# Taps of a depthwise convolution as products on ScalarE and accumulating DMAs, in a kernel of back-to-back matmuls

## The chip, the cores and the metric

The kernel runs on one core of one Trainium2 chip. Five engines of the core matter here, each with its own in-order queue of instructions: TensorE (PE, matmuls, with its weight loads listed as PEld), VectorE (DVE), ScalarE (ACT), GpSimd (POOL) and SyncE (SP, which here only issues DMAs). DMAs can be issued from SP's, ScalarE's and GpSimd's queues; they run on 16 DMA engines that all queues share.

The metric is the device time of one execution in microseconds. The kernel before takes 2484.3 us in the median of 9 runs (2483.25 to 2486.72).

## The reference

Two stages follow each other. `x` is 8 x 4096 x 192, float32; there are 8 heads of 24 channels and 7 taps.

```python
w = softmax(weight, axis=-1)                  # 8 heads x 7 taps
x_pad = concatenate([zeros(B, 6, D), x], 1)   # causal padding of 6 rows
attn[b, s, c] = sum_k w[head(c), k] * x_pad[b, s + k, c]

x2 = attn.reshape(32768, 192)
h = x2 @ w_in                                 # 192 x 2048
g = h * (1 / (1 + exp(-h)))                   # SiLU
out = g @ w_out                               # 2048 x 192
```

The first stage is a small sum of seven shifted and scaled copies of `x` along the sequence. The second is a pair of matrix products over 32768 tokens, and holds nearly all the arithmetic.

## The kernel before, in words

**Blocks and chunks.** The tokens are cut into 32 blocks (`NB`) of 1024. Within a block, the two halves of 512 tokens lie side by side on the partitions: partitions 0 to 63 hold 64 channels of the first half, partitions 64 to 127 the same channels of the second half. The 192 channels are three chunks (`k` = 0, 1, 2) of 64. So a chunk of a block is one tile of 128 partitions x 512 float32, 2 KB a partition.

**From x to the input of the matmuls.** Five steps make the operands of a block:

- `load` (line 123): 12 DMAs on SP bring `x` into the tile `nat`, with tokens on partitions.
- `turn_in` (tokens `i.k` of the plan, line 303): a 32 x 32 block transpose on VectorE, chunk by chunk, from `nat` into `xt`. After the third one, SP issues a small DMA `xt<-xt` that gives the second half its six rows of padding (line 309); GpSimd copies the first half's padding from `tail` (line 300).
- `conv` (tokens `v.ki`: chunk k, tap i; lines 315 to 327): the taps. Tap 0 writes `xt` times the tap's weight into `nat`, whose contents have been transposed already; taps 1 to 6 multiply the shifted `xt` and add to `nat`. All 21 of a block are on VectorE.
- `spread` (line 335): four DMAs a chunk on SP copy each half of `nat` to both halves of the partitions of `dup`, 128 KB each.
- `win` (tokens `w.0` to `w.3`, line 353): four differences of parts of `dup` on VectorE, into `win`.

**The two products.** The kernel saves multiplications with a scheme of the Strassen-Winograd kind over two halves of the tokens, two halves of the hidden columns and two chunks of the channels; the third chunk is multiplied plainly. In the up phase of a block (`product`, line 409), for each of eight column groups m, 11 products go into three PSUM banks. The plan calls them P1 to P7 and E11 to E22, with `P5.0` meaning product P5 of group 0. P1, P6, P7, P4 and E21 add up in one bank, which is read after P1 (`s1`), after P6 (`s2`) and after P7 (`s3`); these copies (`sums_h`, line 424) go to tiles `u`. `C11`, `C12`, `C22` (line 433, VectorE) add a copy and a bank into `g`; `g..` tokens apply SiLU in place (line 430, ScalarE); `C21` is a SiLU straight from the bank (line 428, ScalarE). In the down phase (`down`, line 464), `g` and differences of `g` (`t.ji`, line 450, VectorE) are multiplied by `w_out`. `merge` (tokens M, y, z and c, lines 547 and 550) puts the five result banks together, on ScalarE and VectorE, in `cmb`; `turn_out` (`o.i`, line 559) transposes on VectorE, and four stores a chunk (line 566) follow.

**What sets the order.** The order is written out by hand in `PLAN`: 88 slots separated by `|`, 44 for the up phase and 44 for the down phase, each with two matmuls of TensorE and the work of other engines beside them. `pin` keeps these instructions in the program's order on their engine; the framework adds the waits that data and buffers call for, and places the DMAs and GpSimd's instructions, which are not pinned. Tokens i, v and w in the plan of block b work for block b + 1. A leading minus means the block before. `nat`, `xt`, `dup` and `win` have one buffer each, so `spread` waits until the up phase has read the old `dup`, and `load` for block b + 2 waits until `spread` has read `nat`.

**The first block.** Block 0 is different. Its weights are still being converted from float64 bit patterns by `rounded` on VectorE (line 109), its up phase is plain (`up_plain`, line 373) and its down phase too (`down_plain`, line 503, followed by three copies into `cmb` on ScalarE, line 516). The tokens i, v and w of block 0's plan, which prepare block 1, come in the program after the last call of `rounded` and, those of the second half, within `down_plain`.

Of the kernel before, what the change touches and what calls it, by code (L numbers as in the profile page):

```python
# [9 lines left out]
F32 = mybir.dt.float32  # L10
I32 = mybir.dt.int32
AF = mybir.ActivationFunctionType
ALU = mybir.AluOpType
# [4 lines left out]
def kernel(  # L18
# [24 lines left out]
    nc = tc.nc  # L43
# [6 lines left out]
    P = 128  # L50
    R = 64
    NK = D // R
    grp = D // H
    pad = K - 1
    TB = 512
# [12 lines left out]
    xpool = ctx.enter_context(tc.tile_pool(name="xp", bufs=1))  # L68
# [9 lines left out]

    PLAN = (
        "P1.0 P1.1 -z7.0 -M3.0 | P1.2 P5.0 s1.1 -M4.0 | P5.1 E22.0 s1.0 -M5.0 s1.2 | "  # L80
        "E22.1 P6.1 -M6.0 | P6.0 P1.3 s2.1 | P6.2 P5.2 -o.0 s1.3 s2.0 | P5.3 P7.1 s2.2 | "
        "P7.0 E22.2 -o.1 s3.1 | P7.2 P6.3 i.0 s3.0 C22.1 | E22.3 E21.1 s3.2 s2.3 | "
        "P4.0 P4.1 g22.1 C22.0 | E12.1 P7.3 C22.2 g22.0 | E21.0 E12.0 i.1 C21.1 s3.3 i.2 | "
        "E21.2 E12.2 C21.0 C22.3 | P3.1 P3.0 g22.2 | P4.2 P4.3 g22.3 C12.0 | "
        "E12.3 P2.0 C12.1 g12.0 | P2.1 E11.0 v.00 C21.2 v.01 g12.1 | E11.1 E21.3 C11.0 | "
        "P1.4 P1.5 v.02 C21.3 | P1.6 P3.2 g11.0 C11.1 s1.4 | P3.3 P5.4 C12.2 s1.5 | "
        "P6.4 E22.4 s1.6 C12.3 g11.1 | P5.5 P6.5 s2.4 g12.2 | E22.5 P1.7 v.03 g12.3 s2.5 | "
        "P7.4 P2.2 s1.7 v.04 | P6.6 E11.2 s3.4 v.05 | P2.3 P7.5 C22.4 | "
        "P4.4 P6.7 s2.6 s3.5 C11.2 | E11.3 E12.4 g22.4 s2.7 g11.2 | P7.6 E21.5 C22.5 | "
        "E21.4 P7.7 C11.3 s3.6 | P3.5 P4.5 v.06 g22.5 s3.7 t.00 | E21.6 P3.4 C21.4 | "  # L90
        "E12.5 P4.7 C21.5 t.01 | P4.6 P2.4 g11.3 C12.4 | P5.7 E11.4 C21.6 C12.5 | "
        "E22.7 E21.7 g12.4 C11.4 g12.5 | P2.5 P5.6 C22.7 C21.7 | E11.5 E22.6 t.03 g11.4 | "
        "E12.7 P2.6 g22.7 C22.6 | P3.7 E11.6 C11.5 g22.6 | P2.7 E12.6 v.10 g11.5 C11.6 | "
        "E11.7 P3.6 C12.7 g11.6 | C11.7 g12.7 | C12.6 g11.7 v.11 | g12.6 t.02 | . | v.12 | "
        "v.13 v.14 | v.15 | v.16 | v.20 | t.10 | t.11 | . | t.13 | v.21 | v.22 | v.23 | "
        "t.12 | v.24 | v.25 | v.26 | t.20 | t.21 | . | t.23 | t.22 | t.30 | . | t.31 | w.0 | "
        "w.1 | w.2 | w.3 | t.33 | t.32 | . | . | . | cE.0 | o.2 | y1.0 | z1.0 z6.0 | "
        "z4.0 M2.0 | M1.0 | z5.0"
    )

    def pin(ins):
        return tc.keep_in_program_order(ins)
# [8 lines left out]
    vec = Pinned(nc.vector)  # L111
# [6 lines left out]
    def load(b):  # L118
# [12 lines left out]
        out=wexp.rearrange("p h k -> p (h k)"),  # L131
        in_=weight.rearrange("(o h) k -> o (h k)", o=1).to_broadcast([P, H * K]),
# [5 lines left out]
    for k in range(NK):  # L138
        nc.gpsimd.dma_start(
            out=xts[0][R:P, k, 0:pad], in_=x0[:, k, :], allow_slow_non_contiguous=True  # L140
# [116 lines left out]
    for e in range(2):  # L257
        half = hot[R * e : R * e + R]
        for sign, base in ((1, 0), (-1, grp - 1)):
            nc.gpsimd.affine_select(  # L260
                out=half,
                in_=half,
# [50 lines left out]

    def conv(b, k, i):

        src = xts[b][:, k, i : i + TB]
        dst = nats[b][:, k, :, :].rearrange("p k c -> p (k c)")
        tap = taps[:, k, i : i + 1]
        if i == 0:
            pin(nc.vector.tensor_scalar(dst, src, scalar1=tap, scalar2=None, op0=ALU.mult))  # L320
        else:
            pin(
                nc.vector.scalar_tensor_tensor(  # L323
                    out=dst, in0=src, scalar=tap, in1=dst, op0=ALU.mult, op1=ALU.add
                )
            )

    def spread(b, k):
# [86 lines left out]
    def g_of(b, m, a, n):  # L415
        return g_tile(b, m // 2, a)[:, n, m % 2, :]

    def sums_h(b, name, m):


        if name[0] == "s":
            u = us[b, m, name[1]] = upool.tile([P, TB], F32, tag="u", name="u")
            copy = nc.vector.tensor_copy if name == "s2" else nc.scalar.copy
            pin(copy(u, bk[b, m, "1"]))  # L424
            return
        g = g_of(b, m, int(name[1]) - 1, int(name[2]) - 1)
        if name == "C21":
            pin(nc.scalar.activation(g, bk[b, m, "1"], AF.Silu))  # L428
        elif name[0] == "g":
            pin(nc.scalar.activation(g, g, AF.Silu))  # L430
        else:
            i, bn = {"C11": ("1", "b"), "C22": ("3", "d"), "C12": ("2", "d")}[name]
            pin(nc.vector.tensor_tensor(g, us.pop((b, m, i)), bk[b, m, bn], op=ALU.add))  # L433
# [140 lines left out]
    def step(b, token):  # L574

        if token[0] == "-":
            b, token = b - 1, token[1:]
        name, arg = token.split(".") if "." in token else ("", "")
        if b < 0 or b >= NB or not name or (b, token) in did:
            return  # L580
        did.add((b, token))
        digits = [int(c) for c in arg]
        if name[0] in "PE":
            product(b, digits[0], name)
        elif name[0] in "sCg":
            if b:
                sums_h(b, name, digits[0])
        elif name == "t":
            sum_g(b, *digits)
        elif name[0] in "Mzyc":  # L590
            merge(b, name)
        elif name == "o":
            turn_out(b, *digits)
        elif b + 1 < NB:
            {"i": turn_in, "v": conv, "w": win}[name](b + 1, *digits)
            if name == "v" and digits[1] == K - 1 and (b, "down") in did:
                spread(b + 1, digits[0])
                if digits[0] == NK - 1 and b + 2 < NB:
                    load(b + 2)
# [13 lines left out]
    for k in range(NK):  # L613
        turn_in(0, k)
        for i in range(K):
            conv(0, k, i)
        spread(0, k)
        if k == 0:
            round_in(0)
            load_in(2, nc.gpsimd)  # L620
# [69 lines left out]
```

## Time and profile before

| | |
|---|---|
| median of 9 runs | 2484.3 us (2483.25 to 2486.72) |
| the profiled execution | 2483.94 us, of which the span of the profile is 2482.2 us |
| granted TensorE clock, mean | 0.998 |
| TensorE busy | 2444.1 us, 98% |
| VectorE busy | 2045.5 us, 82% |
| ScalarE busy | 968.1 us, 39% |
| GpSimd busy | 69.9 us, 3% |
| one block, from 1181.92 to 1257.81 us | VectorE 63.3, ScalarE 30.5, GpSimd 1.1 of 75.9 us |
| the same, up phase (38.0 us) alone | VectorE 33.2, ScalarE 25.5 us |
| DMA engines, mean share over the slices of the span | about 0.2 |

The page gives the busy time of every engine; the matmuls are pipelined, so 98% of TensorE is not its peak, but it says that matmuls follow each other. A line of the groups reads: line of the kernel, engine, operation, output and inputs, shapes and count; then total busy time and mean nanoseconds of one; then the idle time of the engine just before these instructions and what ended most of it. A line of the DMA issues gives the queue, the count, the size of one and the median time in microseconds from issue to landing. A line of a timeline gives start, length, engine, line and what was done, merged over a few equal instructions, and in brackets the idle time before and what ended it.

### The profile page before, as it was taken

To read this page: it belongs to the slowest core of one execution; us is meant where nothing else is said; L and a number is where in the kernel's file an instruction comes from. 1 tells how busy PE (TensorE), PEld (TensorE's weight loads), DVE (VectorE), ACT (ScalarE), POOL (GpSimd) and SP (SyncE) were. 2 spreads that over 40 slices of the span, in tenths; PEclk is the share of its full clock that TensorE was granted. 3 is DMA by queue.
4 is the path that set the end of the run, shared out by engine and by line. 5 is a ranking of instruction groups with operands and counts; after the bars stand their busy time and mean duration, and the time that the engine had idled before them with its cause. 6 is when DMAs were issued, how large, how long until landed. Compare 5 with 4: busy or idle time off the path is not lost.

```text
span 2482.2 us, 29776 instructions
## 1 busy us (share of the span) xinstructions
PE 2444.1 (98%) x11296; PEld 959.2 (39%) x11296; DVE 2045.5 (82%) x2748; ACT 968.1 (39%) x1747; POOL 69.9 (3%) x107
## 2 busy tenths in 40 slices
PE   5999999999999999999999999999999999999998
PEld 3334433344333344333443333443334433334432
DVE  8898888888888988888888889888888888898875
ACT  2134433344333344333443333443334433334432
POOL 3300000000000000000000000000000000000000
PEclk9999999999999999999999999999999999999999
DMA  7321122211222211222112222112221122221110
GB/s 148 73 47 31 35 52 51 41 37 35 43 52 43 47 31 35 51 52 41 37 35 43 52 43 47 31 35 52 51 40 38 35 43 52 43 45 32 35 39 13
DMA packets 450270, 110.78 MB, mean 45 GB/s; under 512 B 422304, under 2 KB 423968, under 8 KB 450128
## 3 DMA queue, kind: packets, MB, share of 16 engines
q1 hardware_dynamic: 444272, 101.26, 21.4%
q0 software_dynamic: 1600, 4.92, 0.8%
q10 hardware_dynamic: 4256, 2.72, 0.5%
q8 instruction: 88, 1.44, 0.2%
q14 instruction: 54, 0.44, 0.1%
HBM read 31.49 MB, written 25.17 MB: 23 GB/s over the span
## 4 chain that ended last, share of the span: by engine, by line
PE 97%; DVE 2%; DMA 1%; issue 0%; POOL 0%; ACTq 0%; ACT 0%; POOLq 0%; DVEq 0%
PE ps L409 47%; PE ps L464 47%; PE ps L503 2%; PE ps L373 1%; DVE two L109 1%; DVE nat L323 0%; DMA nat<-in_x_dram 0%; DMA raw<-in_moe_w_in_dram 0%; DVE mh L109 0%; DVE xt L303 0%; POOL raw L163 0%; DVE nat L320 0%; DVE u L550 0%; DVE cmb L550 0%; ACTq L217 0%
## 5 line engine op out<-in xcount | busy, mean ns | idle before, releaser
L464 PE MATMUL ps<-g,wo 128*64 128x512 f32 x2976 | 873.2, 593 | 0.0
L409 PE MATMUL ps<-dup,ws 64*128 64x512 f32 x2480 | 869.9, 589 | 0.0
L433 DVE TENSOR_TENSOR g<-u,ps 128x512 f32<-128x512 f32 x744 | 489.2, 681 | 116.6 <-PE ps L409 102.8
L409 PE MATMUL ps<-win,wr 64*128 64x512 f32 x1488 | 567.7, 589 | 0.0
L464 PEld LDWEIGHTS ps<-g,wo 128*64 128x64 f32 x2976 | 275.6, 137 | 572.2 <-issue 548.7
L430 ACT ACTIVATE g<-g 128x512 f32<-128x512 f32 x744 | 445.5, 631 | 88.2 <-DVE g L433 88.2
L409 PEld LDWEIGHTS ps<-dup,ws 64*128 64x128 f32 x2480 | 363.1, 187 | 291.9 <-issue 284.6
L464 PE MATMUL ps<-t,wx 128*64 128x512 f32 x992 | 466.2, 592 | 0.0
L323 DVE SCALAR_TENSOR_TENSOR nat<-xt,taps,nat 128x512 f32<-128x512 f32 x576 | 431.8, 750 | 11.9
L547 ACT COPY cmb<-ps 64x512 f32<-64x512 f32 (+1 forms) x93 | 54.0, 581 | 965.1 <-PE ps L464 964.3
L409 PE MATMUL ps<-dup,wr 64*128 64x512 f32 x992 | 420.0, 596 | 0.0
L424 ACT COPY u<-ps 128x512 f32<-128x512 f32 x496 | 277.7, 588 | 233.6 <-PE ps L409 233.3
L464 PE MATMUL ps<-t,wo 128*64 128x512 f32 x992 | 360.6, 592 | 0.0
L450 DVE TENSOR_TENSOR t<-g,t 128x1024 f32<-128x1024 f32 x248 | 303.6, 1224 | 60.4 <-PE ps L464 49.9
L409 PEld LDWEIGHTS ps<-win,wr 64*128 64x128 f32 x1488 | 233.5, 187 | 175.3 <-issue 146.9
L450 DVE TENSOR_TENSOR t<-g 128x1024 f32<-128x1024 f32 x248 | 299.6, 1219 | 0.0
L409 PE MATMUL ps<-win,ws 64*128 64x512 f32 x496 | 242.2, 589 | 0.0
L464 PE MATMUL ps<-g,wx 128*64 128x512 f32 x496 | 233.1, 592 | 0.0
L409 PEld LDWEIGHTS ps<-dup,wr 64*128 64x128 f32 x992 | 160.5, 187 | 127.3 <-issue 120.0
L424 DVE COPY u<-ps 128x512 f32<-128x512 f32 x248 | 166.5, 681 | 12.0 <-PE ps L409 8.2
L428 ACT ACTIVATE g<-ps 128x512 f32<-128x512 f32 x248 | 143.9, 595 | 79.5 <-PE ps L409 75.6
L559 DVE STREAM_TRANSPOSE osb<-cmb 128x512 f32<-128x512 f32 x96 | 67.5, 704 | 86.9 <-ACT cmb L547 79.0
(57 smaller groups left out, 1090.4 us busy)
## 6 DMA issues: line engine op xcount, KB each, us to landing
dup<-nat SPq DMA_DIRECT2D x384, 128.0 KB, 2.3
nat<-in_x_dram SPq DMA_DIRECT2D x382, 64.0 KB, 2.4
out_dram<-osb SPq DMA_DIRECT2D x378, 64.0 KB, 1.9
raw<-in_moe_w_out_dram POOLq DMA_DIRECT2D x8, 384.0 KB, 4.2
raw<-in_moe_w_in_dram POOLq DMA_DIRECT2D x8, 192.0 KB, 5.7
ws<-wr ACTq DMA_DIRECT2D x8, 192.0 KB, 4.7
raw<-in_moe_w_in_dram ACTq DMA_DIRECT2D x4, 192.0 KB, 5.8
raw<-in_moe_w_in_dram SPq DMA_DIRECT2D x4, 192.0 KB, 3.7
```

The costliest lines, as they stand in the source:

```text
L109: return lambda *args, **kw: pin(getattr(self.engine, name)(*args, **kw))
L323: nc.vector.scalar_tensor_tensor(out=dst, in0=src, scalar=tap, in1=dst, op0=ALU.mult, op1=ALU.add)
L409: nc.tensor.matmul(bk[b, m, bn], rows(w, half), rows(v, half), start=first, stop=True, skip_group_check=True,)
L424: pin(copy(u, bk[b, m, "1"]))
L428: pin(nc.scalar.activation(g, bk[b, m, "1"], AF.Silu))
L430: pin(nc.scalar.activation(g, g, AF.Silu))
L433: pin(nc.vector.tensor_tensor(g, us.pop((b, m, i)), bk[b, m, bn], op=ALU.add))
L450: pin(nc.vector.tensor_tensor(t[i // 2][:, i % 2, :], u, v, op=ALU.subtract))
L464: nc.tensor.matmul(accs[b][i][R * half : R * half + R, :], lhs, rhs, start=first and j == 0, stop=j == NJ - 1, skip_group_check=True,)
L503: nc.tensor.matmul(acc[k][R * n : R * n + R, :], wo[j][:, a, e, R * k : R * k + R], gs[b, j, a][:, n, e, :], start=j == 0 and a == 0 and e ...
L547: pin(nc.scalar.copy(*copies[name]()))
L559: nc.vector.transpose(osb[:, i, :, :].rearrange("p k c -> p (k c)"), cmbs[b][0][:, i, :])
```

## The change

For all blocks but the first, the taps leave VectorE. Each product of a tap is an ACTIVATE on ScalarE (a copy with the tap's weight as scale of each partition). Tap 0 still writes `nat`; the products of taps 1 to 6 go into a new tile `prod` of 128 x 512 float32 with three buffers, and a DMA issued from GpSimd's queue adds `prod` to `nat` (256 KB each, 18 a block). Block 0 keeps its taps on VectorE.

The copy `s3`, one for each of the eight column groups, moves from ScalarE to VectorE, where `s2` is already.

The plan is written anew around this: same matmuls in the same slots, other places for the rest. The taps go by rounds through the three chunks (v.00, v.10, v.20, v.01, v.11, ...) instead of chunk after chunk; they begin in slot 28 instead of 17 and end in slot 71 instead of 63. The transposes `i` move from slots 8 to 12 to slots 17 to 25, the stores `-o.0` and `-o.1` from slots 5 and 7 to 14 and 15, the windows `w` from slots 72 to 75 to slots 82 to 84, `o.2` from 82 to 87; many C, g and t tokens shift by some slots, and M1 and M2 change places.

```diff
-        "E22.1 P6.1 -M6.0 | P6.0 P1.3 s2.1 | P6.2 P5.2 -o.0 s1.3 s2.0 | P5.3 P7.1 s2.2 | "
-        "P7.0 E22.2 -o.1 s3.1 | P7.2 P6.3 i.0 s3.0 C22.1 | E22.3 E21.1 s3.2 s2.3 | "
...
-        "E12.3 P2.0 C12.1 g12.0 | P2.1 E11.0 v.00 C21.2 v.01 g12.1 | E11.1 E21.3 C11.0 | "
...
-        "v.13 v.14 | v.15 | v.16 | v.20 | t.10 | t.11 | . | t.13 | v.21 | v.22 | v.23 | "
-        "t.12 | v.24 | v.25 | v.26 | t.20 | t.21 | . | t.23 | t.22 | t.30 | . | t.31 | w.0 | "
-        "w.1 | w.2 | w.3 | t.33 | t.32 | . | . | . | cE.0 | o.2 | y1.0 | z1.0 z6.0 | "
-        "z4.0 M2.0 | M1.0 | z5.0"
+        "P3.1 P3.0 g22.2 -o.0 g22.3 | P4.2 P4.3 -o.1 C12.0 | E12.3 P2.0 C21.2 C12.1 | "
+        "P2.1 E11.0 g12.0 i.0 g12.1 | E11.1 E21.3 C11.0 | P1.4 P1.5 i.1 C21.3 | "
...
+        "P5.5 P6.5 g11.1 s2.4 g12.2 | E22.5 P1.7 s2.5 g12.3 | P7.4 P2.2 i.2 s1.7 | "
+        "P6.6 E11.2 s3.4 | P2.3 P7.5 C22.4 s2.6 | P4.4 P6.7 s3.5 v.00 | "
+        "E11.3 E12.4 s2.7 v.10 | P7.6 E21.5 C22.5 v.20 v.01 C11.2 | E21.4 P7.7 v.11 s3.6 | "
+        "P3.5 P4.5 v.21 s3.7 | E21.6 P3.4 C21.4 C11.3 C21.5 t.00 | E12.5 P4.7 g11.2 | "
...
+        "P2.5 P5.6 C22.7 v.02 | E11.5 E22.6 C11.4 v.12 | E12.7 P2.6 v.22 C22.6 C21.7 | "
...
+        "C12.7 g11.6 C11.7 | g12.7 C12.6 | v.03 t.02 | v.13 v.23 t.10 | g11.7 | g12.6 t.11 | "
+        "g22.6 g22.7 | . | . | . | v.04 t.13 v.14 | v.24 t.12 | . | t.20 | t.21 | . | . | "
+        ". | v.05 v.15 | v.25 | . | t.23 | t.22 | . | t.30 | t.31 v.06 | v.16 | v.26 | . | "
+        ". | . | . | t.33 | t.32 | . | . | . | cE.0 | w.0 w.1 | y1.0 w.2 | z1.0 w.3 z6.0 | "
+        "z4.0 M1.0 | M2.0 | o.2 z5.0"
...
     def conv(b, k, i):
         src = xts[b][:, k, i : i + TB]
         dst = nats[b][:, k, :, :].rearrange("p k c -> p (k c)")
         tap = taps[:, k, i : i + 1]
-        if i == 0:
-            pin(nc.vector.tensor_scalar(dst, src, scalar1=tap, scalar2=None, op0=ALU.mult))
+        if b:
+            out_ = dst
+            if i:
+                out_ = xpool.tile([P, TB], F32, tag="prod", name="prod", bufs=NK)
+            pin(nc.scalar.activation(out_, src, AF.Copy, scale=tap))
+            if i:
+                nc.gpsimd.dma_start(out=dst, in_=out_, accum_op=ALU.add)
+        elif i == 0:
+            vec.tensor_scalar(dst, src, scalar1=tap, scalar2=None, op0=ALU.mult)
         else:
-            pin(
-                nc.vector.scalar_tensor_tensor(
-                    out=dst, in0=src, scalar=tap, in1=dst, op0=ALU.mult, op1=ALU.add
-                )
+            vec.scalar_tensor_tensor(
+                out=dst, in0=src, scalar=tap, in1=dst, op0=ALU.mult, op1=ALU.add
             )
...
             u = us[b, m, name[1]] = upool.tile([P, TB], F32, tag="u", name="u")
-            copy = nc.vector.tensor_copy if name == "s2" else nc.scalar.copy
+            copy = nc.vector.tensor_copy if name != "s1" else nc.scalar.copy
             pin(copy(u, bk[b, m, "1"]))
```

## The prediction

> **What bounds the kernel now.** I read the page first: busy times, then the chain that ended last.
>
> ```profile
> PE 2444.1 (98%) x11296; PEld 959.2 (39%) x11296; DVE 2045.5 (82%) x2748; ACT 968.1 (39%) x1747; POOL 69.9 (3%) x107
> PE 97%; DVE 2%; DMA 1%; issue 0%; POOL 0%; ACTq 0%; ACT 0%; POOLq 0%; DVEq 0%
> ```
>
> TensorE is the bound: 97% of the chain is its own work. Then the chain in order of time (start, length, what):
>
> ```profile
> 78.19 41.35 PE ps L503 x192
> 119.53 37.97 PE ps L409 x176
> 157.50 37.92 PE ps L464 x176
> ```
>
> From 78.19 us on, matmul phases follow each other without a gap: 41.35 us of down products of block 0, then 37.97 + 37.92 = 75.89 us for each of blocks 1 to 31. A phase is 44 slots of the plan, 0.862 us each. No relief of VectorE can shorten this stretch; the change can only leave it alone or open gaps in it. What matters is whether `dup` of the next block is there when its products start. In steady state there are 75.89 us to make it. In block 0 there are not, so I read VectorE's timeline there:
>
> ```profile
> 88.88 0.96 DVE L109 SCALAR_TENSOR_TENSOR wo<-mh,two 128x768 f32<-128x768 f32 x1
> 89.76 1.89 DVE L303 STREAM_TRANSPOSE xt<-nat 128x512 f32<-128x512 f32 x3
> 93.71 0.48 DVE L320 TENSOR_SCALAR nat<-xt,taps 128x512 f32<-128x512 f32 x1 [2.06 <-DMA xt<-xt]
> ...
> 104.47 4.69 DVE L323 SCALAR_TENSOR_TENSOR nat<-xt,taps,nat 128x512 f32<-128x512 f32 x6
> 109.08 0.69 DVE L353 TENSOR_TENSOR win<-dup 128x512 f32<-128x512 f32 x1
> ...
> 112.54 0.68 DVE L353 TENSOR_TENSOR win<-dup,win 128x512 f32<-128x512 f32 x1
> ```
>
> VectorE rounds weights until 89.8 us, so the taps of block 1 can't start before 93.7. All 21 take it 15.4 us, to 109.1; the windows are ready at 113.2, and TensorE wants them at 119.5. The spare time is 6.3 us. Groups and DMA issues give the prices:
>
> ```profile
> L323 DVE SCALAR_TENSOR_TENSOR nat<-xt,taps,nat 128x512 f32<-128x512 f32 x576 | 431.8, 750 | 11.9
> L424 ACT COPY u<-ps 128x512 f32<-128x512 f32 x496 | 277.7, 588 | 233.6 <-PE ps L409 233.3
> L424 DVE COPY u<-ps 128x512 f32<-128x512 f32 x248 | 166.5, 681 | 12.0 <-PE ps L409 8.2
> L430 ACT ACTIVATE g<-g 128x512 f32<-128x512 f32 x744 | 445.5, 631 | 88.2 <-DVE g L433 88.2
> ```
> ```profile
> dup<-nat SPq DMA_DIRECT2D x384, 128.0 KB, 2.3
> out_dram<-osb SPq DMA_DIRECT2D x378, 64.0 KB, 1.9
> out_dram<-osb POOLq DMA_DIRECT2D x3, 64.0 KB, 3.0
> ```
>
> The last figure is the time from issue to landing: from the Pool queue it is 1.1 us longer for the same 64 KB.
>
> **What the Trainium skill says.** "DMA: Bandwidth & Descriptors", section "SWDGE vs HWDGE vs iDMA": only GpSimd issues accumulating DMAs. No run here has one. Its section "Two DMAs through the same engine are not ordered": a DMA that depends on an earlier one has to be held until that one's completion count is there. So the six additions to one chunk are a chain of full landings, not a stream. The present kernel chains no DMAs, so the trace neither confirms nor contradicts this.
>
> **The change part by part.** Per block after the first:
>
> 1. *VectorE loses the taps*: 18 x 0.750 + 3 x 0.484 (the L320 group) = 14.95 us. It gains the eight `s3` copies: 8 x 0.681 = 5.45 us. Net -9.5 us of 63.3 busy us a block. Worth nothing: TensorE's phases already touch.
>
> 2. *ScalarE loses eight copies* (8 x 0.588 = 4.7 us) and gains 21 products. "ScalarE: Activation LUTs", section "What ACT_TABLE_LOAD costs", gives 186 ns + 0.833 ns an element, 93 ns more for a per-partition scale, and 93 ns of overlap back to back: 0.71 us alone, 0.61 in a row. The trace agrees in kind: 0.631 for a 512-wide ACTIVATE from SBUF. So 21 x 0.61 = 12.8 us; ScalarE goes from 30.5 to about 39 of 75.9 us. Hidden.
>
> 3. *GpSimd gains 18 DMA issues*, 0.73 us each by the present weight loads (0.72 to 0.76): 13 us of a nearly idle engine.
>
> 4. *The chain.* Let T be the time from an accumulating DMA's issue to its landing. A chunk's next product waits for its `prod` buffer (three buffers, one in use by each chunk), so one tap of one chunk takes T + 0.71 + about 0.1 for two handovers = T + 0.8.
> T isn't in the trace. Lower bound, by the price of "DMA: Bandwidth & Descriptors", "Anatomy of one DMA — SWDGE path" (about 2.0 us fixed, and bytes at 436 GB/s): an estimate of 2.6 us for 256 KB. The trace is above that price on the Pool queue: 3.0 against 2.15 for 64 KB; 3.7 against 2.9 for the 384 KB weight loads between 66 and 78 us, when nothing else moved. A plain 256 KB should thus take about 3.4 us. An accumulation reads the destination too. A 2 KB packet of `dup` took 0.14 us of an engine (28.4% of 16 engines for 20 us, some 640 packets); 128 packets on 16 engines are 1.15 us, and as much again if the second read costs like the first. That gives 4.5 us; three such DMAs of the three chunks overlap and partly queue, for which I add 0.3. I take T = 4.8. Upper bound: three times the packet time, with the three DMAs in file, 3 x 3.4 = 10 us a round.
>
> 5. *Block 1, the path that sets the end.* Transposes and the small `xt` DMA stay where they are, so products start at 93.7. Three first products, then v.01 ends at 93.7 + 3 x 0.61 + 0.71 = 96.2. Six rounds: the last sum of chunk 0 lands at 96.3 + 6T + 5 x 0.8 = 100.3 + 6T; the other two chunks follow within 1.5 us. Behind it SP issues twelve `dup` DMAs at 0.596 us each (its timeline), the last 6.6 us after the first, landing 2.3 us later: 109.2 + 6T. The sixth product, E22.0, needs that one; before, it ran at 119.5 + 5 x 0.431 = 121.6. The gap is 6T - 12.4 = 16.4 us at T = 4.8. The first five products run inside the wait. ScalarE's three `cmb` copies of block 0 stand behind the products; they free three PSUM banks that these five products don't need.
>
> 6. *Steady blocks.* Measured from the block's start: the third transpose stands in slot 25 (21.6 us) and takes 0.7, the small `xt` DMA 2.1, so the first product runs at 24.4 us and v.01 ends at 26.9. The same chain gives 26.9 + 0.1 + 6T + 4.0 + 8.9 = 39.9 + 6T for the last `dup`, against 75.9 + 2.1 = 78.0 for E22.0. It is hidden up to T = 6.35; at 4.8 there are 9 us to spare. Behind a product that waits stand ScalarE's activations; from slot 50 to slot 81 it has none but products, so a late tap hurts nobody else. At nothing: cover is those 9 us; if it goes, each us of T costs 6 us a block.
>
> 7. *Moves.* Transposes go from slots 8-12 to 17-25; `load` of the following block now ends near 79 us, 2.7 us into the next block, and is wanted at 14.7: hidden, 12 us spare. The stores of o.0 and o.1 go eight to nine slots later on SP, where only the small `xt` copies stand behind them. Windows go to slots 82-84; w.3 is first wanted in slot 10 of the next block. `s3` on VectorE takes 0.09 us longer and has two to four slots before P4 wants its bank; VectorE's up half stays as full as it was (eight taps out, 5.5 us; eight copies in, 5.45). In the last block o.2 stands behind M2, and its ScalarE-queue store may hold up the two last copies: 0 to 0.8 us, I take 0.4.
>
> Sum: 16.4 + 0.4 = +16.8 us. On the profiled execution (span 2482.2, 2483.94 with what lies around) that is a span of 2499.0; the median of the runs is 0.4 above that execution, so 2484.3 + 16.8 = 2501.1 us.
>
> **The rivals.** *The chain outlasts the block* (T above 6.35): all 30 later blocks stall before E22.0. At T = 7: 29.6 + 0.4 + 30 x 6 x 0.65 = +147 us, 2631 us. For it: unknown price, three DMAs sharing 16 engines. Against: engines are 20% busy, and nearly idle in the slots concerned.
> *Not slower: the additions land fast.* Same place, block 1; decides at 6T - 12.4 below 5, T under 2.9. At the skill's 2.6: +3 us, 2487.5. Against: the trace's Pool DMAs all sit 0.8 above that price, without a second read.
> *VectorE late with `s3`*: eight copies 0.09 us longer, all exposed, 31 blocks: +23 us on top, 2524. Against: the slots counted in 7.
>
> **How the numbers follow.** Likeliest case 0.74 (T from 2.9 to 6.35), stalls in every block 0.17, hidden 0.06, `s3` 0.03. About 0.2% (5 us) is what a measurement here can tell from no change. Faster 0.01, same 0.06, slower 0.93. Low end: T = 3.2, +6.8: 2491. High end: T = 6.5, 26.6 + 0.4 + 30 x 6 x 0.15 = +54: about 2540. Some 0.05 lies below and 0.14 above.
>
> **What would show it.** One gap in TensorE's matmuls, near 121 us and some 16 us long, released by `dup`, with VectorE idle and ScalarE waiting for accumulations; after it phases of 75.9 us again; accumulations landing in 4 to 6 us; VectorE near 1750 us busy. Gaps at every block would prove the first rival; a start of block 1's products at 119.5 the second; waits on L424 copies the third.

## The result, and the profile after

The changed kernel takes 2499.99 us in the median of 9 runs (2498.72 to 2501.36), against 2484.28 us for the kernel before (29 runs): a ratio of 1.0062, 95% interval 1.0053 to 1.0070. The profiled execution took 2499.12 us, with a span of 2497.4 us, 15.2 us more than the span before. (Line numbers are six higher than before from `conv` on: L415 is the up phase, L470 the down phase. Taps that stay on VectorE are now issued through a helper and carry its line, L109.)

The page of the changed kernel, busy times and the chain that ended last by engine:

```profile
PE 2448.8 (98%) x11296; PEld 974.3 (39%) x11296; DVE 1771.4 (71%) x2345; ACT 1255.0 (50%) x2150; POOL 542.9 (22%) x665
PE 94%; DVE 3%; DMA 2%; issue 1%; SPq 0%; POOL 0%; ACT 0%; ACTq 0%; POOLq 0%; DVEq 0%
```

VectorE lost 274 us of work and the kernel got slower. TensorE's share of the chain went from 97% to 94%; 1.7 of these points are the down phase of block 0 (41.4 us), beside which the chain now runs through VectorE and DMAs. The chain in order of time shows where nothing changed:

```profile
170.31 37.92 PE ps L470 x176
208.23 37.97 PE ps L415 x176
...
2408.89 37.97 PE ps L415 x176
```

From block 2 on, the phases have the lengths of before, and they touch: (2408.89 - 208.23) / 29 = 75.89 us a block, as before. All of the loss lies ahead of 170.31 us, where the down phase of block 1 starts 12.8 us later than its 157.50, and behind the last matmul. TensorE's timeline, early part:

```profile
80.10 41.42 PE L509 MATMUL ps<-g,wo 128*64 128x512 f32 x192
127.43 3.78 PE L415 MATMUL ps<-dup,wr 64*128 64x512 f32 x6 [5.91 <-DMA dup<-nat]
131.02 1.45 PE L415 MATMUL ps<-win,ws 64*128 64x512 f32 x4
134.00 1.13 PE L415 MATMUL ps<-dup,ws 64*128 64x512 f32 x4 [1.52 <-DMA dup<-nat]
```

TensorE waits for `dup` twice: for P1.0 until 127.43, and for E22.0 until 134.00. VectorE's timeline, to be read against the one of before:

```profile
90.22 1.89 DVE L303 STREAM_TRANSPOSE xt<-nat 128x512 f32<-128x512 f32 x3
130.18 0.69 DVE L359 TENSOR_TENSOR win<-dup 128x512 f32<-128x512 f32 x1 [38.07 <-DMA dup<-nat]
```

It transposes block 1 where it did before and then has nothing to do for 38 us, until `dup` is there. What fills these 38 us is the chain of waits (start, length, what; "issue" is time in which the engine waited for nothing that the profile shows):

```profile
104.28 3.54 DMA nat<-prod
...
107.90 0.73 ACT prod L324
108.63 0.28 issue
108.92 4.01 DMA nat<-prod
...
131.63 2.33 DMA dup<-nat
133.95 0.04 issue
134.00 6.27 PE ps L415 x27
```

Landing, product, 0.3 us of handing over, landing: that is one round of the chain. The products of chunk 0 start at 96.0, 100.45, 104.76, 109.51, 114.27 and 119.05, so a round takes 4.61 us. The page's DMA issues and groups give the prices that were unknown:

```profile
nat<-prod POOLq DMA_DIRECT2D x558, 256.0 KB, 3.7
dup<-nat SPq DMA_DIRECT2D x384, 128.0 KB, 2.9
```
```profile
L326 POOL DMA_DIRECT2D nat<-prod x558 | 482.8, 970 | 1796.6 <-ACT prod L324 1775.5
L324 ACT ACTIVATE prod<-xt,taps 128x512 f32<-128x512 f32 x558 | 384.5, 716 | 234.9 <-DMA nat<-prod 233.7
```

An accumulating DMA of 256 KB lands 3.7 us after its issue in the median (3.5 in block 1, 3.2 at the least). A product takes 0.716 us. ScalarE waits 234 us in all for landings; after block 1 no phase of TensorE gets longer by it.

At the end of the kernel, TensorE finishes at 2408.89 + 37.97 + 37.92 = 2484.78, and the span ends 12.6 us later; before it was 10.2 us. ScalarE's timeline of the last block:

```profile
2482.31 0.58 ACT L553 COPY cmb<-ps 64x512 f32<-64x512 f32 x1
2484.26 0.38 ACTq L572 DMA_DIRECT2D out_dram<-osb  x1
2484.74 1.18 ACT L553 COPY u<-ps 64x512 f32<-64x512 f32 x2 [1.84 <-DVE osb L565]
```

The store of o.2 waits on ScalarE's queue for the transpose, and z5 and z7 wait behind it: the last adds start 1.2 us after TensorE's end instead of 0.6. The other 1.8 us are the drain of GpSimd's queue, in the listing of the kernel's last line (min, median and max in ns), here and in the kernel before:

```profile
L691 POOLq DRAIN  x3: 46/102/6124, 2490.5 to 2497.1; - x3
```
```profile
L685 POOLq DRAIN  x3: 46/93/4317, 2477.1 to 2482.0; - x3
```

12.8 + 0.6 + 1.8 = 15.2 us: the whole difference of the spans.

### The profile page after: what moved, and what is told of

Same layout as the page of the kernel before. It is cut to its first block, busy times and chain, and to the rows that moved or that the text cites. A ratio compares the mean times of both kernels' runs of the same rounds, so it can differ in the third digit from the quotient of the medians.

```text
span 2497.4 us, 31928 instructions
## 1 busy us (share of the span) xinstructions
PE 2448.8 (98%) x11296; PEld 974.3 (39%) x11296; DVE 1771.4 (71%) x2345; ACT 1255.0 (50%) x2150; POOL 542.9 (22%) x665
## 4 chain that ended last, share of the span: by engine, by line
PE 94%; DVE 3%; DMA 2%; issue 1%; SPq 0%; POOL 0%; ACT 0%; ACTq 0%; POOLq 0%; DVEq 0%
PE ps L415 47%; PE ps L470 47%; DVE two L109 1%; DMA nat<-prod 1%; DVE nat L109 1%; DVE mh L109 0%; DMA raw<-in_moe_w_in_dram 0%; DMA nat<-in_x_dram 0%; SPq L341 0%; DVE wo L109 0%; ACT prod L324 0%; DMA dup<-nat 0%; DVE xt L303 0%; DVE u L556 0%; POOL raw L163 0%
## 5 line engine op out<-in xcount | busy, mean ns | idle before, releaser
L326 POOL DMA_DIRECT2D nat<-prod x558 | 482.8, 970 | 1796.6 <-ACT prod L324 1775.5
L470 PE MATMUL ps<-g,wo 128*64 128x512 f32 x2976 | 873.2, 593 | 0.0
L415 PE MATMUL ps<-dup,ws 64*128 64x512 f32 x2480 | 868.0, 589 | 1.5 <-DMA dup<-nat 1.5
L415 PE MATMUL ps<-win,wr 64*128 64x512 f32 x1488 | 568.1, 589 | 0.0
L324 ACT ACTIVATE prod<-xt,taps 128x512 f32<-128x512 f32 x558 | 384.5, 716 | 234.9 <-DMA nat<-prod 233.7
L470 PEld LDWEIGHTS ps<-g,wo 128*64 128x64 f32 x2976 | 275.6, 137 | 572.2 <-issue 544.2
L436 ACT ACTIVATE g<-g 128x512 f32<-128x512 f32 x744 | 423.9, 624 | 115.6 <-DVE g L439 113.7
L415 PEld LDWEIGHTS ps<-dup,ws 64*128 64x128 f32 x2480 | 362.0, 187 | 292.3 <-issue 269.2
L470 PE MATMUL ps<-t,wx 128*64 128x512 f32 x992 | 466.2, 592 | 0.0
L415 PE MATMUL ps<-dup,wr 64*128 64x512 f32 x992 | 420.2, 599 | 5.9 <-DMA dup<-nat 5.9
L430 DVE COPY u<-ps 128x512 f32<-128x512 f32 x496 | 338.8, 689 | 51.4 <-PE ps L415 37.4
L470 PE MATMUL ps<-t,wo 128*64 128x512 f32 x992 | 360.6, 592 | 0.0
L415 PEld LDWEIGHTS ps<-win,wr 64*128 64x128 f32 x1488 | 234.0, 187 | 174.5 <-issue 166.7
L415 PE MATMUL ps<-win,ws 64*128 64x512 f32 x496 | 240.8, 591 | 0.0
L470 PE MATMUL ps<-g,wx 128*64 128x512 f32 x496 | 233.1, 592 | 0.0
L415 PEld LDWEIGHTS ps<-dup,wr 64*128 64x128 f32 x992 | 160.1, 187 | 126.6 <-issue 111.4
L430 ACT COPY u<-ps 128x512 f32<-128x512 f32 x248 | 133.2, 592 | 109.9 <-PE ps L415 109.9
```

The source lines that it names most:

```text
L324: pin(nc.scalar.activation(out_, src, AF.Copy, scale=tap))
L326: nc.gpsimd.dma_start(out=dst, in_=out_, accum_op=ALU.add)
L415: nc.tensor.matmul(bk[b, m, bn], rows(w, half), rows(v, half), start=first, stop=True, skip_group_check=True,)
L470: nc.tensor.matmul(accs[b][i][R * half : R * half + R, :], lhs, rhs, start=first and j == 0, stop=j == NJ - 1, skip_group_check=True,)
```

## The experiments

The theory: only block 1 lies open, because its taps can't start before VectorE has finished the weights; steady blocks hide their chain; the plan and `s3` cost nothing. The rivals: a cost in every block, from the chain or from `s3`.

**Block 1 back on VectorE.**

```diff
-        if b:
+        if b > 1:
             out_ = dst
```

> The changed kernel, but block 1 keeps its taps on VectorE as block 0 does; blocks 2 to 31 have products on ScalarE and accumulating DMAs. Theory (only block 1's chain lies open, steady blocks hide theirs): the gap before E22.0 is gone, block 1's products start within 0.5 us of where they did before (39 us after the start of the down phase of block 0), later blocks stay at 75.9 us, and what is left is the end of the kernel (about 2.4 us: the two copies behind the store of o.2, and a longer drain of GpSimd's queue): 2484.3 + 2.4 = 2486.7 us. Rival (the chain also costs something in every steady block, or s3 does): more than 2490 us.

Measured: 2486.63 us, 1.0007 of the kernel before (0.9998 to 1.0015). Each ratio is to the kernel before as timed beside that run; here that was 2486.05 us. In the chain of this run, block 1's products follow the down phase of block 0 (78.54 + 41.35 = 119.89) at once:

```profile
119.89 37.97 PE ps L415 x176
157.86 37.92 PE ps L470 x176
```

One block out of 31 gives back 13.4 of the 15.7 us (13.7 of 15.4 by the two ratios). The other 30, with 540 accumulating DMAs, cost nothing that can be told from zero. This settles where the loss was.

**The end of the kernel.** The same, with `o.2` back in slot 82:

```diff
-        if b:
+        if b > 1:
...
-        ". | . | . | t.33 | t.32 | . | . | . | cE.0 | w.0 w.1 | y1.0 w.2 | z1.0 w.3 z6.0 | "
-        "z4.0 M1.0 | M2.0 | o.2 z5.0"
+        ". | . | . | t.33 | t.32 | . | . | . | cE.0 | o.2 w.0 w.1 | y1.0 w.2 | z1.0 w.3 z6.0 | "
+        "z4.0 M1.0 | M2.0 | z5.0"
```

> The changed kernel with block 1's taps on VectorE and o.2 back in slot 82, before the windows. Against the run with block 1 on VectorE alone: the two copies z5 and z7 no longer stand behind o.2's store on ScalarE's queue in the last block, so the first of the last adds starts 0.63 us after TensorE's end instead of 1.2: 0.5 us less, about 2486.1 us on a chip where the kernel before takes 2484.5. What stays is GpSimd's drain at the end (5.4 us instead of 4.3). If the tail had another cause, this changes nothing.

Measured: 2485.70 us, 1.0005 of the kernel before (0.9997 to 1.0013). That is 0.9 us under the last run, but their intervals overlap; the place is shown by the trace. TensorE ends at 2434.01 + 37.94 = 2471.95, and the last adds start at 2472.58, 0.63 us later, as before the change. GpSimd's drain still takes 5.4 us. The two terms of the tail are thus the store ahead of the copies and the drain. No version of the study is faster than the kernel before; from 78 us on, TensorE's phases touched already, so relief of VectorE had nothing to shorten there.

**What a round of the chain is.** Two runs. In the first, block 1's products go to the 13 tiles `u`, so the products run ahead and none waits for a landing:

```diff
-                out_ = xpool.tile([P, TB], F32, tag="prod", name="prod", bufs=NK)
+                if b == 1:
+                    out_ = upool.tile([P, TB], F32, tag="u", name="prod")
+                else:
+                    out_ = xpool.tile([P, TB], F32, tag="prod", name="prod", bufs=NK)
```

> The changed kernel, but in block 1 the products of taps 1 to 6 go into the pool of 13 tiles u instead of the three tiles prod, so that no product waits for a landing and only the additions to one chunk are a chain. If a round of block 1 (4.63 us) is landing plus product, as the prediction's T + 0.8 has it: a round falls to about 3.7 us, six rounds save about 5 us, some 2495 us. If a round is what the 16 DMA engines need for three accumulations (0.96 busy in that stretch: 4.4 us): less than 1.5 us saved, 2498.5 to 2500 us.

Measured: 2499.52 us, 1.0056 (1.0042 to 1.0070). The 18 issues span 25.1 us (96.59 to 121.66) instead of 26.1 (97.02 to 123.16): a round falls by 0.2 us, not by 0.9. The DMA view of its stretch from 95 to 130 us says why:

```profile
q0 software_dynamic: 2592, 4.72, 76.7%
...
nat<-prod POOLq DMA_DIRECT2D x18, 256.0 KB, 4.2
```

The accumulations take 76.7% of 16 engines for 35 us, 1.49 us of all engines each; three need 4.47 us. With products out of the way the landing grows from 3.5 to 4.2 us, and a round (25.1 / 17 x 3 = 4.4 us) is about what the engines need for three. In the second run, chunk 0 goes alone:

```diff
-        if b:
+        if b > 1 or b == 1 and k == 0:
             out_ = dst
```

> The changed kernel, but in block 1 only chunk 0 goes by products and accumulating DMAs; chunks 1 and 2 stay on VectorE. It measures one chain by itself. If a round is landing plus product (landing of a lone accumulation 3.2 us, the least seen; product 0.72; two handovers 0.3): 4.2 us a round, v.06's sum lands near 94.2 + 0.7 + 6 x 4.2 = 120 us, block 1 starts 5 us late: about 2492 us. If a round were only what the DMA engines need (1.5 us for one accumulation): six rounds take 9 us, no gap at all, 2486.7 us. With both this and the run with 13 buffers, a round is the larger of landing plus product and three times 1.5 us.

Measured: 2490.79 us, 1.0022 (1.0015 to 1.0030). ScalarE's and GpSimd's timelines, and block 1's landings:

```profile
94.24 1.94 ACT L324 ACTIVATE prod<-xt,taps 128x512 f32<-128x512 f32 x3
```
```profile
99.13 0.89 POOL L326 DMA_DIRECT2D nat<-prod  x1 [1.93 <-DMA nat<-prod]
102.94 0.85 POOL L326 DMA_DIRECT2D nat<-prod  x1 [2.92 <-DMA nat<-prod]
107.72 0.85 POOL L326 DMA_DIRECT2D nat<-prod  x1 [3.94 <-DMA nat<-prod]
```
```profile
DMA to landing us min/median/max: 3.2/3.3/4.3
```

The six issues start between 95.26 and 115.99 us: five rounds in 20.7 us, 4.15 each, where 4.2 was expected. But this agreement is luck. With three buffers for one chain, three products are done before the first landing, and each later issue waits for the landing before it and not for a product. A round is thus landing plus handing over (about 0.5 us), without the product: 3.7 to 3.9 us in three rounds, 4.5 and 4.8 in two, whose landings take 4.25 us while the `dup` copies of the other two chunks run beside them. Block 1's first product starts 2.05 us late rather than 5: the last sum lands at 119.2 us, and that product needs only the first of the four copies behind it. With the windows, block 1's down phase starts 3.6 us later than in the run with block 1 on VectorE.

So two limits lie close together: the 4.47 us that the DMA engines need for three accumulations, and landing, product and handing over one after another, an estimate of 4.4 us from the pieces above (3.3 + 0.7 + 0.4); no run has a lone chain with the product in its round. The changed kernel's three chains and three buffers have both, and its round took 4.61 us. Which of the two sets it is not isolated; removing the product alone gained 0.2 us.

**How much steady blocks have to spare.** Each product with half the weight, added twice, which gives the same sum:

```diff
+    half = const.tile([P, NK, K], F32, name="half")
+    vec.tensor_scalar(half, taps, scalar1=0.5, scalar2=None, op0=ALU.mult)
...
+            twice = 0 < i          # second run: 0 < i < 3
+            if twice:
+                tap = half[:, k, i : i + 1]
             pin(nc.scalar.activation(out_, src, AF.Copy, scale=tap))
             if i:
-                nc.gpsimd.dma_start(out=dst, in_=out_, accum_op=ALU.add)
+                for _ in range(2 if twice else 1):
+                    nc.gpsimd.dma_start(out=dst, in_=out_, accum_op=ALU.add)
```

> The changed kernel with each product of taps 1 to 6 computed with half the weight and added twice, by two accumulating DMAs one behind the other; the sum is the same. The chain of a block grows by 6 landings of about 3.6 us, 21.6 us. Theory (block 1 open, steady blocks with some 9 us to spare, and about 3 us of slack between the first rounds): 21.6 us more in block 1, and 9 us or more in each of 30 steady blocks, 2790 us and more; the prediction's own formula (39.9 + 6T at T = 7.4 against 78.0) gives 6.3 us a block, 2710 us. Rival (steady blocks are not near a limit): 2521 us.

Measured: 3084.0 us, 1.2406 (1.2384 to 1.2429). Here every block stalls, for `dup`, and by more than I had written: E22.0 starts at 1289.08 + 2.33 and 1385.06 + 2.35, 96 us a block, 20 us over. The DMA engines' time explains most of it: 18 x 1.49 = 26.8 us more a block, less the 10 us that a steady block of the changed kernel has to spare (its last `dup` has landed by 1262.4 us, E22.0 starts at 1272.4), is 16.8. Another 2.8 us go with TensorE's clock, below: from E22.0 to the next block's first product it takes 25.6 us instead of 22.8. My estimate had counted landings one after another, with 9 us or more as a lower end; its formula with T gave 6.3 us and was too low, because it counted the landings of one chain and not the time that the DMA engines need for three. With taps 1 and 2 alone doubled:

> The changed kernel with taps 1 and 2 added in two halves, by two accumulating DMAs each (half the weight, the sum is the same); the other taps as they are. Six more accumulations a block, 6 x 1.49 = 8.9 us more of the DMA engines. Theory (steady blocks have 9 to 10 us to spare): only block 1 gets longer, 2500.0 + 8.9 = 2509 us, and later blocks stay at 75.9 us. If steady blocks have less to spare: 30 us more for each us that is lacking.

Measured: 2518.43 us, 1.0132 (1.0110 to 1.0154): 18.4 us over the changed kernel, not 9. In block 1, E22.0 starts at 143.54 instead of 134.00, 9.5 us later; six more accumulations should cost 6 x 1.49 = 8.9. Two things were not foreseen. The up phase after the wait took 38.23 us instead of 36.31, with the granted clock at 0.50 from 127 to 147 us. And 12 of the 30 steady up phases are longer, by up to 1.1 us, 7.9 us in all, though `dup` is not what they wait for. TensorE's waits between 230 and 2480 us:

```profile
PEld ps L422 <- DVE u L437: 19.1, 67, 0.8
PEld ps L477 <- ACT prod L330: 17.7, 29, 0.8
...
PEld ps L422 <- DMA dup<-nat: 4.3, 6, 0.8
```

In the same stretch of the changed kernel the first two are 14.1 and 2.9 us. In one of the long blocks, ScalarE stands for 2.9 us before the product of tap 2 (at 2387.78), with the activations of the last groups behind it. That fits, but no run isolates it, so which waits make up the 7.9 us is left open. For `dup`, steady blocks do have room for 9 us; for ScalarE's queue they have less.

**The plan and `s3` by themselves.** The new plan and `s3` on VectorE, but no accumulating DMA in any block (`if b > NB:` in place of `if b:`):

> The new plan and s3 on VectorE, but all taps on VectorE in every block; no accumulating DMA. Theory (the plan and s3 are harmless): 2484.3 + 0.5 = 2484.8 us, the 0.5 being the two copies that wait behind o.2's store in the last block; the drain at the end is as short as before (4.3 us instead of 6.1). Rival (VectorE, fuller by 5.5 us a block, is late for the accumulation banks): 0.1 to 0.7 us a block, 2488 to 2507 us.

Measured: 2582.19 us, 1.0388 (1.0374 to 1.0402). Neither of my numbers: 3.2 us in every block. The chain shows VectorE back to back at the end of the up phase (start, length, what):

```profile
1148.09 22.57 PE ps L415 x104
1170.66 0.68 DVE u L430
...
1175.23 1.06 DVE nat L109 x2
1176.29 0.60 DVE g L439
1176.89 0.66 DVE nat L109
```

(Here `nat` on L109 is a tap.) For 17 us TensorE goes at VectorE's pace. The new plan puts nine taps into slots 28 to 40, between copies and adds that free TensorE's banks; on ScalarE they harm nobody, on VectorE they stand in the way. To see how much of it is `s3`, the same with `s3` on ScalarE (`name == "s2"`):

> The new plan with all taps on VectorE, as in the run that took 2582 us, but with s3 on ScalarE. If s3 made that run slow (5.5 us more work for VectorE in an up phase that was full): 2485 us. If it is the nine taps which the new plan puts into the last 16 slots of the up phase: 2530 us or more; nine taps are 6.2 us there against eight in the whole up phase before, so I expect a part of each, about 2500 us.

Measured: 2538.58 us, 1.0213 (1.0191 to 1.0235), more than the 2500 that I had leaned to: with this plan, `s3` makes 44 us of the 98. The other 54 belong to the rest of the new plan with the taps on VectorE; the chain above points at the place of the taps, but the plan's other moves were not run apart. And the changed kernel itself, with `s3` back on ScalarE alone:

> The changed kernel with s3 back on ScalarE. Theory (s3 costs nothing while the taps are off VectorE, and ScalarE has room): 2500.0 us, within 1 us. Rival (s3 on VectorE delays banks): faster by 3 us or more.

Measured: 2513.83 us, 1.0115 (1.0099 to 1.0131): slower by 14 us, where I expected no difference, and against the rival as well. TensorE's waits have an entry that the changed kernel has not, and ScalarE's timeline shows the place:

```profile
PEld ps L415 <- ACT u L430: 31.5, 61, 1.0
```
```profile
2295.78 1.94 ACT L324 ACTIVATE nat<-xt,taps 128x512 f32<-128x512 f32 x3
2297.63 1.32 ACT L324 ACTIVATE prod<-xt,taps 128x512 f32<-128x512 f32 x2
2298.86 0.57 ACT L430 COPY u<-ps 128x512 f32<-128x512 f32 x1
```

Five products in a row stand ahead of the copy, 3.1 us, and TensorE wants its bank. The up phase is 38.4 us instead of 37.97, 0.45 us a block. So moving `s3` is what makes room for the products in this plan. The parts hold each other up: the plan without the products costs 54 us, the products without `s3`'s move 14. What the products or `s3` would do under the old plan was not run.

## Why the prediction was right, and where its sum was not

It said 2501.1 us; the kernel takes 2500.0. Step by step:

- **The bound** held: phases of 75.89 us from block 2 on, in both kernels.
- **Step 1**, VectorE's relief worth nothing: 54.6 busy us a block instead of 63.3 (8.7 less for the 9.5 worked out), and not one of them shows in a phase.
- **Step 2**, ScalarE: 39.6 busy us a block against "about 39". But "hidden" was right only because `s3` had left: the run with `s3` back on ScalarE pays 14 us. I had gone by the share and not by five products in a row.
- **Step 3**: 0.86 us an issue in most cases rather than 0.73; it stays hidden.
- **Step 4**, the price T, is the term that was mis-sized: 4.8 us assumed, 3.3 for one chain and 3.5 in block 1 measured. A 2 KB packet of an accumulation costs 0.19 us of an engine (76.6% of 16 engines for 35 us, 18 x 128 packets) against 0.14 for `dup`, or 1.49 us of all engines for 256 KB against 1.13; so the second read that I had charged in full, with 1.15 us, costs 0.36. Against the estimate of 2.6 us for 256 KB from the Trainium skill, "DMA: Bandwidth & Descriptors", "Anatomy of one DMA — SWDGE path", the least landing was 3.2: the step's reasoning that the Pool queue lies above that price held, the surcharge on top of it did not. A round was 4.61 us instead of 5.6. Its form, T + 0.8, was only half the story: without the product, in the run with 13 buffers, a round was still 4.4, by the DMA engines' time. Over five rounds and the last landing this is 6.2 us less; the first addition was issued 0.7 us later (97.0 for 96.3), so the last sum of chunk 0 landed 5.5 us earlier (123.6 for 129.1).
- **Step 5**, the place, was right. From the first `dup` issue to the last landing it took 10.4 us, not 8.9: one issue took 1.63 us instead of 0.60 while the last accumulations still filled the DMA engines (0.97 busy from 123 to 127 us). So E22.0 started at 134.0 where I had 138.0. Block 1's later matmuls add 0.5 us with the clock.
- **The last part of step 7**, the end of the kernel: 2.4 us instead of 0.4. The store on ScalarE's queue was foreseen (0.6 us, inside 0 to 0.8); the drain of GpSimd's queue, 1.8 us, was not in the sum, a term put at nothing without a reason.
- **Step 6**, steady blocks hidden with 9 us to spare: right as to `dup`, as the run with two taps doubled shows. Its slope of 6 us a block for each us of T was not, since beyond the limit the DMA engines' own time counts. And that a late tap hurts nobody else was argued for slots 50 to 81 only; taps stand in slots 38 to 40 too, with activations behind them, and in that run 12 up phases got longer.
- **The rivals**: no stall in every block, no block 1 on time. The one on `s3` was not only absent but the wrong way round.

That the sum, 16.8 us, came so near to the 15.2 us between the spans is partly luck: the rounds were 6.2 us too dear, while the start (0.7), the copies (1.5), the clock (0.5) and the end of the kernel (2.0) were together 4.7 us too cheap.

In two of the eleven profiles of this study (this one and the run with all taps doubled) the down phase of block 0 starts at 80.1 and 80.3 us instead of 78.1 to 78.6, here after a slow stretch of TensorE's clock at 58 to 66 us (0.75 and 0.82). It did not add to the result here: block 1 waited for its taps anyway.

## What to carry to other kernels

Before moving work off a busy engine, look for the stretch where its result is awaited soonest. In this kernel, whose bound engine never stops later on, that was the start. Price a chain of dependent DMAs there by its rounds (landing plus whatever has to be done between two landings, or the DMA engines' time for all chains together, whichever is longer) and not by busy time. Where such a chain is right for the steady part, let the first block keep the short way. And price an in-order queue by what stands in a row ahead of the urgent instruction: half-idle ScalarE was late after five products, in the run with `s3` back on it.

## What was not expected of the hardware

After its stall in block 1, TensorE ran slower for a while. The granted clock in stretches of 4 us, of the changed kernel (stretch, its length, busy times, then the clock behind the engines, DMA share, GB/s):

```profile
123.00:127.00 4.00, 0.00 (x0) 0.00 (x0) 0.00 (x0) 1.31 (x3) 1.87 (x4) 0.74 0.97 162
127.00:131.00 4.00, 3.57 (x6) 1.09 (x7) 0.69 (x1) 0.00 (x0) 0.00 (x0) 0.50 0.94 236
131.00:135.00 4.00, 2.48 (x12) 1.06 (x12) 2.52 (x4) 1.56 (x3) 0.00 (x0) 0.91 0.55 130
```

It had 1.00 just before, and 1.00 again from 135 us. In the run with block 1 on VectorE, TensorE doesn't stop and the clock is 1.00 in all these stretches. The price is 0.5 us here and 2.2 us in the run with 13 buffers (36.31 and 38.04 us from E22.0 to the down phase; these 166 of 176 matmul records take 37.97 x 166 / 176 = 35.8 at the pace of the kernel before), where the clock stood at 0.50 from 123 to 135 us. With a stall in every block, TensorE's busy time grew from 2448.8 to 2600.6 us for the same 11296 records, and the mean clock fell to 0.904: some 5 us of TensorE's time a stall. No rule on how long a stand it takes comes out of these runs: in the run with one chain TensorE stands for 2.05 and 0.82 us, and the clock stays at 1.00; in the profile of the changed kernel a stand of 1.83 us just before 59.9 us goes with 0.75 from 58 to 62 us, in the kernel before one of 1.27 us with 1.00.

The drain of GpSimd's queue at the end took 4.3 and 4.9 us in the two runs of new plans without accumulating DMAs (4.3 in the kernel before), 5.4 with 540, 6.1 with 558, 5.9 with 744 and 8.1 with 1116. It is longer with them in every run, but not in step with their number, and its cause stays open.
